# Block-sparse attention and a rational-activation MLP on one core: one written order for all engines through step 13, x split straight out of PSUM, and some pieces moved

## Chip, cores and metric

The kernel runs on 1 core of one Trainium2 chip. The metric is the device time of one execution in microseconds (us), median of the runs; lower is better. TensorE is called PE, VectorE DVE, ScalarE ACT, GpSimd POOL, and SyncE, which issues most transfers, SP.

## Reference

```python
B, H, S, D = 4, 8, 768, 64
block, window = 32, 16
k_sum = k.reshape(B, H, nb, block, D).max(axis=3)       # nb = 24 blocks
v_sum = v.reshape(B, H, nb, block, D).mean(axis=3)
scores_l = scale * q @ k.T, masked to |i - j| < window
scores_s = scale * q @ k_sum.T + log(block)
a = softmax(concat([scores_l, scores_s]))
attn = a @ concat([v, v_sum])
x = attn.transpose(0, 2, 1, 3).reshape(B * S, H * D)     # 3072 x 512
h = x @ w_in                                             # 512 -> 2048
g = (a0 + a1*h + a2*h*h + a3*h*h*h) / (1 + |b0|*|h| + |b1|*h*h + 1e-6)
return g @ w_out                                         # 2048 -> 512
```

## The kernel before

**Attention.** The 3072 rows are cut into 48 halves of 64 queries (`HQ`). One half covers all 8 heads, as 4 pairs (`NPAIR`). For a half, `scores` multiplies 64 queries with 96 neighbouring keys and 24 block keys, on quarters of the PE array (64x64); DVE adds the mask and takes the minimum (tile `ss`), ACT does four exponentials with their sums, DVE a reciprocal, POOL four multiplications (`ss<-ss,sm`). `turned` transposes on PE (tile `pt`), ACT or DVE copies to `pts`, and `values` multiplies with the values (tile `av`). From half 16 on, two halves go together (`both_scores`, `both_values`), and the transposition goes through memory (`crossed`).

**MLP.** Eight halves make a group of 512 rows, so there are six groups; a group has 16 steps, one for each 128 columns of the hidden layer. Step n does `moe1` (12 matmuls of 512 columns into tile `h`), the activation in `gelu`, and `moe2` of step n-3 (`LAG`; 12 matmuls into the four tiles `po`). Numbers are split in a high and a low part (`xh`/`xl`, the two parts of `wearly` and `w`, `gh`/`gl`), and three products of parts are added. In `gelu`, ACT makes a square, an absolute value and a line of `h`; DVE makes `tu` and `tq`; ACT does a logarithm and an exponential; DVE makes `gh` and the rest; POOL makes `gl`. `h` lies in a PSUM pool of two buffers (`ps_h`), which DVE's second product (`tu<-tu,cs,h`) reads last; scores, transposes and `av` of halves from 8 on, and ACT's squares of some steps, share another pool of two (`ps_a`).

**Weights.** They arrive packed; `w_split` unpacks them in the first group in five parts: ACT, POOL, DVE (`wr<-wr`), ACT's copy of the high part, and DVE's subtraction for the low part.

**The x of a group.** In group 0, `values` writes `xh` and `xl` from PSUM. In later groups ACT copies `av` to an fp32 tile `x` and `split`, at the first step of the group, makes `xh` (ACT) and `xl` (DVE) from it.

**Order.** `Kept` ties the instructions of an engine in the order of the program text while the engine is in `strict`. Before, PE, DVE, ACT and POOL are; SP is not. The text up to step 13 comes from three lists: `FIRST` (loads), `EARLY` (halves 0 to 7 and the first weights) and `STEP`, a pattern repeated for steps 0 to 13. From step 14 (`NSTRICT`) on, PE stays in the order of the text and the others are placed by the scheduler.

Of the kernel before, what the change touches and what calls it, by code (L numbers as in the profile page):

```python
# [8 lines left out]
F32 = mybir.dt.float32  # L9
# [38 lines left out]
FIRST = "K0 Q0 K1 K2 K3 Q1 S F W0 V0 V1 V6 V2 V4 V5 A9 W1 V7 V3 A8 W2 W3 G"  # L48
EARLY = "s0 s1 e0 s2 s6 e1 s3 s4 P0 v0 v1 e2 e3 e4 v2 v3 s5 P1 v4 v5 w0 w0 e5 w0 s7 P2 m0 w0 w0 C0 e6 P4 P3 e7 c2 c1 k8 p5 P6 C3 w1 P7 w1 c5 c4 w1 c6 c7 k9 w1 w1 w2 w2"
# [6 lines left out]
STEP = "k0 h3 w1 h2 h0 w2 P2 w1 w3 h3 g1 h0 g0 l0 q0 g1 g0 q0 h1 w2 u h0 a0 w3 v g0 h2"  # L56
# [4 lines left out]
def tile_kernel(ctx, tc, qw_in, kraw, kwin, vpad, vred, wio, a, b, cmask, cident, cavg, out):  # L61
# [36 lines left out]
    pe, dve, act, gps = Kept(nc.tensor), Kept(nc.vector), Kept(nc.scalar), Kept(nc.gpsimd)  # L98
# [11 lines left out]
    const.tile([P, 96], F32, name="shift")  # L110
    wearly = const.tile([P, NSTG, 2, 2, DM], F32R, name="wearly")
    const.tile([P, 32], F32, name="shift2")
# [6 lines left out]
    def setup():  # L119
# [5 lines left out]
        dve.tensor_scalar_mul(cs[:, 6:7], cs[:, 5:6], -1.0)  # L125
        dve.tensor_tensor(cs[:, 5:6], cs[:, 5:6], cs[:, 6:7], op=ALU.max)
        dve.memset(cs[:, 7:8], C1 * SH)

    ksum, vsum, att, x32, prods = {}, {}, {}, {}, {}
# [3 lines left out]
    def key_load(bi, pr):  # L133
        if pr == 0:
            ksum[bi] = sp.tile([P, NPAIR, NB], F32, tag="ks", name=f"ks{bi}", bufs=2)
        if bi == 0:
            nc.sync.dma_start(out=kres[:, pr, :], in_=kraw[bi, pr])
            kr = kres[:, pr, WIN:WIN + S]
        else:
            kr = stage.tile([P, S], F32, tag="st", name=f"kr{bi}_{pr}")  # L140
            nc.sync.dma_start(out=kr, in_=kraw[bi, pr, :, WIN:WIN + S])
        sums["k", bi, pr] = kr

    def key_sum(bi, pr):
        kr = sums.pop(("k", bi, pr))
        ins = dve.tensor_reduce(ksum[bi][:, pr, :], kr.rearrange("p (n k) -> p n k", k=BLK), axis=AX.X, op=ALU.max)
        if bi:
            tc.keep_in_program_order(ins)

    def value_load(bi, c):  # L150
# [3 lines left out]
        nc.sync.dma_start(out=vr, in_=vred[bi, c])  # L154
# [8 lines left out]
    def value_tiles(bi):  # L163
        vt = []
        for i, (n, pool, tag) in enumerate(((4, xp, "x" if bi else "xh"), (2, stage if bi else xp, "st" if bi else "xl"))):
            t = pool.tile([P, n, DM], F32, tag=tag, name=f"vf{bi}_{i}")
            nc.sync.dma_start(out=t, in_=vpad[bi, WIN + 4 * i * P:WIN + (4 * i + n) * P, :].rearrange("(t p) e -> p t e", p=P))
            vt += [t[:, k, :] for k in range(n)]
        return vt

    def value_average(av, vt, i):
        pe.matmul(av[:NK, :], avg[:, AVGW - NK - 4 * i:AVGW - 4 * i], vt[i], start=(i == 0), stop=(i == len(vt) - 1))

    def first_means(av):
        for t in vres[0:3]:
# [4 lines left out]
    def second_means(av):  # L180
        t = pp.tile([NK, DM], F32, tag="p", name="vn")
        act.copy(t[NKW:NK, :], av[NKW:NK, :])
        nc.sync.dma_start(out=vnext, in_=t[NKW:NK, :])

    def first_q(lo, hi):
        nc.sync.dma_start(out=qres[:, lo:hi], in_=qw_in[0, lo:hi].rearrange("j p r q -> p j r q"))

    def att_load(jj):
        bi, j = divmod(jj, NJ)
        nc.sync.dma_start(out=qw[jj % 2], in_=qw_in[bi, j])  # L190
        nc.sync.dma_start(out=kw[jj % 2][:, 0:NKC - 1], in_=kwin[bi, j])

    def key_blocks(jj):
        bi, j = divmod(jj, NJ)
        if j < 2 and bi > 0 or jj in (HPG, HPG + 1):
            dve.tensor_copy(kw[jj % 2][:, NKC - 1], ksum[bi])

    def both_scores(j0):

        tiles = [ps_a.tile([P, 512], F32, tag="a", name=f"sc{j0 + k}") for k in range(2)]  # L200
        for pr in range(NPAIR):
            for k in range(2):
                for e in range(2):
                    rows, q = slice(e * D, (e + 1) * D), e ^ k
                    pe.matmul(tiles[k][q * HQ:(q + 1) * HQ, pr * NK:(pr + 1) * NK], qw[k][rows, pr, :],
                              kw[k][rows, :, pr, :], start=True, stop=True)
        return tiles

    def scores(jj, early=False, sc=None):

# [475 lines left out]
```

## Time and profile before

| | us |
|---|---|
| median of 3 runs | 647.54 (644.51 to 650.65) |
| the profiled execution | 645.66 |
| its span | 643.6 |
| PE busy | 623.1 (97%) |
| DVE busy | 573.3 (89%) |
| ACT busy | 459.1 (71%) |
| POOL busy | 259.7 (40%) |

The span is the stretch that the trace covers; 2.06 us of the profiled execution lie around it. A busy PE counts also matmuls that run at a lower granted clock. A row of the timeline gives start, duration, engine, line, operation, output and inputs, count, and in brackets the idle time of the engine before it with what ended it. A row of the groups gives count, busy time, mean in ns, and idle time.

### The profile page before, as it was taken

The numbers are of one execution on the slowest core, as the hardware profiler recorded it, in microseconds if no ns is written. First come the engines' busy times: TensorE is split into PE (matmuls) and PEld (weight loads), VectorE is DVE, ScalarE is ACT, GpSimd is POOL, SyncE is SP. The second block draws the span as 40 slices with busy tenths as digits, with TensorE's granted clock in tenths as the row PEclk, the third lists the DMA queues.
The fourth block names the chain that finished last, engine by engine and source line by source line (L and its number), as shares of the span: only waits on it lengthen the run. The fifth ranks groups of instructions, "written<-read, shape, count | busy, mean of one in ns | idle before, by whom it ended". The sixth has DMA issues, their size and how long they took to land.

```text
span 643.6 us, 11833 instructions
## 1 busy us (share of the span) xinstructions
PE 623.1 (97%) x4068; PEld 497.2 (77%) x4068; DVE 573.3 (89%) x1152; ACT 459.1 (71%) x1032; POOL 259.7 (40%) x350
## 2 busy tenths in 40 slices
PE   8897999999999999999999999999999999999997
PEld 5564776777788887788887888888788888888886
DVE  5789999999988999998999999888988888898885
ACT  3987988978767667866767876767867756755552
POOL 1838569664243244333333245333334232222221
PEclk9997999999999999999999999999999999999999
DMA  8997854304443434244334343323233110100001
GB/s 314 301 346 253 256 190 148 134 27 133 144 145 125 143 111 141 66 141 143 115 110 132 92 134 105 93 72 121 66 130 124 31 64 1 44 22 1 0 2 65
DMA packets 51559, 77.00 MB, mean 120 GB/s; under 512 B 6068, under 2 KB 33076, under 8 KB 49580
## 3 DMA queue, kind: packets, MB, share of 16 engines
q1 hardware_dynamic: 50796, 75.80, 36.6%
q8 instruction: 32, 0.52, 0.3%
q10 hardware_dynamic: 576, 0.25, 0.2%
q0 software_dynamic: 128, 0.20, 0.1%
q14 instruction: 27, 0.22, 0.1%
HBM read 61.31 MB, written 14.73 MB: 118 GB/s over the span
## 4 chain that ended last, share of the span: by engine, by line
PE 62%; DVE 19%; POOL 7%; ACT 5%; issue 4%; DMA 2%; SPq 0%; DVEq 0%; POOLq 0%
PE po L88 28%; PE h L88 27%; DVE tu L88 7%; POOL ss L88 5%; DVE tq L88 4%; PE sc L88 3%; PE av L88 3%; DVE gh L88 2%; DVE xl L88 2%; ACT ta L88 1%; PE vf L88 1%; DVE ss L88 1%; DMA kres<-in_kraw_dram 1%; POOL gl L88 1%; ACT ss L88 1%
## 5 line engine op out<-in xcount | busy, mean ns | idle before, releaser
L88 POOL TENSOR_TENSOR gl<-tu,ta 128x512 fp32r<-128x512 f32 x96 | 129.4, 1348 | 311.3 <-DVE tu L88 156.9
L88 POOL TENSOR_SCALAR ss<-ss,sm 128x120 f32<-128x120 f32 x192 | 100.8, 544 | 61.8 <-DVE sm L88 59.1
L88 ACT ACTIVATE ta<-tq,cs 128x512 f32<-128x512 f32 x96 | 69.6, 725 | 77.1 <-DVE tq L88 75.8
L88 PE MATMUL po<-wearly,gh 128*128 128x512 f32 x384 | 121.6, 398 | 0.0
L88 PE MATMUL po<-w,gh 128*128 128x512 f32 x384 | 120.6, 395 | 0.0
L88 PE MATMUL h<-xh,wearly 128*128 128x512 f32 x384 | 97.2, 395 | 0.5 <-ACT xh L88 0.5
L88 PE MATMUL h<-xh,w 128*128 128x512 f32 x384 | 94.9, 389 | 0.0
L88 PEld LDWEIGHTS h<-xh,wearly 128*128 128x128 f32 x384 | 72.6, 189 | 17.6 <-issue 2.0
L88 PEld LDWEIGHTS h<-xh,w 128*128 128x128 f32 x384 | 72.0, 188 | 15.2 <-ACT x L88 0.2
L88 PEld LDWEIGHTS po<-w,gh 128*128 128x128 f32 x384 | 70.7, 188 | 15.3 <-issue 1.3
L88 PEld LDWEIGHTS po<-wearly,gh 128*128 128x128 f32 x384 | 70.0, 189 | 15.4 <-issue 1.7
L88 ACT ACTIVATE ss<-ss,sm 128x120 f32<-128x120 f32 x192 | 73.2, 386 | 12.1 <-DVE sm L88 12.0
L88 DVE SCALAR_TENSOR_TENSOR gh<-tu,cs,ta 128x512 fp32r<-128x512 f32 x96 | 72.6, 757 | 9.7 <-ACT ta L88 1.6
L88 DVE SCALAR_TENSOR_TENSOR tu<-tu,cs,tq 128x512 f32<-128x512 f32 x96 | 72.9, 759 | 2.4
L88 PE MATMUL po<-w,gl 128*128 128x512 f32 x192 | 74.9, 390 | 0.0
L88 PE MATMUL po<-wearly,gl 128*128 128x512 f32 x192 | 74.9, 390 | 0.0
L88 ACT ACTIVATE tu<-h,cs 128x512 f32<-128x512 f32 x96 | 74.8, 779 | 0.0
L88 DVE SCALAR_TENSOR_TENSOR tu<-tu,cs,h 128x512 f32<-128x512 f32 x96 | 71.4, 743 | 2.3
L88 DVE SCALAR_TENSOR_TENSOR tq<-tq,gh 128x512 f32<-128x512 f32 x96 | 66.7, 695 | 3.1
L88 ACT ACTIVATE ta<-h,cs 128x512 f32<-128x512 f32 x96 | 65.3, 680 | 3.0 <-POOL gl L88 2.9
L88 DVE TENSOR_TENSOR tu<-tu,h 128x512 f32<-128x512 f32 x96 | 65.0, 677 | 0.3 <-ACT tu L88 0.3
L88 ACT ACTIVATE ta<-ta 128x512 f32<-128x512 f32 x96 | 60.8, 634 | 2.8
(73 smaller groups left out, 918.2 us busy)
## 6 DMA issues: line engine op xcount, KB each, us to landing
wr<-in_wio_dram SPq DMA_DIRECT2D x15, 1024.0 KB
cross<-tb SPq DMA_DIRECT2D x32, 256.0 KB
vw<-in_vpad_dram SPq DMA_DIRECT2D x42, 192.0 KB
kw<-in_kwin_dram SPq DMA_DIRECT2D x40, 192.0 KB
pts<-cross SPq DMA_DIRECT2D x96, 64.0 KB
out_dram<-o SPq DMA_DIRECT2D x24, 256.0 KB
qw<-in_qw_dram SPq DMA_DIRECT2D x40, 128.0 KB
kr<-in_kraw_dram SPq DMA_DIRECT2D x12, 384.0 KB
```

The source lines that it names most:

```text
L88: out = getattr(self.engine, name)(*args, **kw)
```

## The change

1. `FIRST`, `EARLY` and `STEP` become one list, `TEXT`, whose tokens name single parts: `h8` the next part of half 8, `x2` the next third of `moe1` of step 2, `y1` the next quarter of `moe2`, `ga3` to `gk3` parts of the activation of step 3, `w`, `W`, `V`, `K` and so on weights and loads. SP is kept in the order of the text too.
2. In all groups `xh` and `xl` are written from PSUM, with two buffers each; `x` and `split` go.
3. `both_scores` also does halves 0 and 1, 2 and 3, 8 and 9 (`PAIRS`).
4. For the weights of steps 5, 7 and 8 (`MODE` e) the low part is made by ACT's negative of the high part and an adding transfer that POOL issues, in place of DVE's subtraction.
5. In half 3 (`SMODE` y) POOL subtracts the minimum, ACT does one exponential over all four pairs and DVE the sums.
6. In steps 1 to 15 `moe1` multiplies with the low weights last.

```diff
-FIRST = "K0 Q0 K1 K2 K3 Q1 S F W0 V0 ...
-EARLY = "s0 s1 e0 s2 s6 e1 s3 s4 P0 ...
-STEP = "k0 h3 w1 h2 h0 w2 P2 w1 w3 h3 g1 h0 ...
+TEXT = ("K0 K2 k0 Q0 K1 k1 k2 K3 k3 Q1 S0 F0 W0 ...
+PAIRS = "11001000"
+SMODE = "xxxyxxxxxxxxxxxx"
+ENG_P = "dddddaadaaadaaaa"
+ENG_X = "daadaaaaaaadaaaa"
+MODE = "ccccceceeccccccc"
...
@@ values
-        if g:
-            act.copy(x32[g][:, :, cols], av)
-        else:
-            xh, xl = x32[0]
-            (dve.tensor_copy if jj in by_dve else act.copy)(xh[:, :, cols], av)
-            yield
-            dve.tensor_tensor(xl[:, :, cols], av, xh[:, :, cols], op=ALU.subtract)
+        xh, xl = x32[g]
+        (dve.tensor_copy if ENG_X[jj] == "d" else act.copy)(xh[:, :, cols], av)
+        yield
+        dve.tensor_tensor(xl[:, :, cols], av, xh[:, :, cols], op=ALU.subtract)
...
@@ both_values
-        act.copy(x32[g][:, :, hh * HQ:(hh + 2) * HQ], av.rearrange("p r k q -> p r (k q)"))
-
-    def split(g):
...
-        for c in range(NCC):
-            act.copy(xh[:, c], x32[g][:, c])
-            dve.tensor_tensor(xl[:, c], x32[g][:, c], xh[:, c], op=ALU.subtract)
+        xh, xl = (x[:, :, hh * HQ:(hh + 2) * HQ] for x in x32[g])
+        av = av.rearrange("p r k q -> p r (k q)")
+        act.copy(xh, av)
+        dve.tensor_tensor(xl, av, xh, op=ALU.subtract)
...
@@ w_split
+            whole = packed.bitcast(F32)
+            if mode == "e":
+                act.copy(wt[:, 0], whole)
...
+            if mode != "a":
+                act.mul(wt[:, 1], wt[:, 0], -1.0)
...
+                gps.dma_start(out=wt[:, 1], in_=whole, accum_op=ALU.add)
...
@@ moe1
-        for i, x in ((0, xh), (1, xh), (0, xl)):
+        for i, x in ((0, xh), (0, xl), (1, xh)) if 0 < g * NFC + fc < NFC else ((0, xh), (1, xh), (0, xl)):
```

Three places show how the instructions move. The first is PE around `moe2` of step 2, with the transposes of half 10 (`pt_1010` before, `pt_1021` now). Before:

```order
L88 MATMUL h_5_987<-xl_464,wearly 128x512 x4
L88 MATMUL pt_1010<-ident,ss_870 120x128
L88 MATMUL po_0_844<-wearly,gh_2_757 128x512 x2
L88 MATMUL po_0_844<-wearly,gl_2_758 128x512
L88 MATMUL pt_1010<-ident,ss_870 120x128
L88 MATMUL po_1_845<-wearly,gh_2_757 128x512 x2
```

Now:

```order
L105 MATMUL po_2_819<-wearly,gh_2_753 128x512 x2
L105 MATMUL po_2_819<-wearly,gl_2_754 128x512
L105 MATMUL po_3_820<-wearly,gh_2_753 128x512 x2
L105 MATMUL po_3_820<-wearly,gl_2_754 128x512
L105 MATMUL pt_1021<-ident,ss_879 120x128 x4
L105 MATMUL h_6_1048<-xh_452,wearly 128x512 x4
```

The four transposes stood one ahead of each quarter of `moe2`; now they stand together behind all four. The second place is DVE at the start of group 1, in the activation of steps 14 and 15 (`tu_14`, `tq_15`). Before, it holds the four subtractions of `split`:

```order
L88 SCALAR_TENSOR_TENSOR tq_14_1689<-tq_14_1689,gh_14_1686 128x512
L88 TENSOR_TENSOR xl_1835<-x_817,xh_1834 128x512
L88 SCALAR_TENSOR_TENSOR tu_14_1690<-tu_14_1690,cs,tq_14_1689 128x512
L88 TENSOR_TENSOR xl_1835<-x_817,xh_1834 128x512 x2
L88 STREAM_TRANSPOSE tb_1804<-ss_1721 128x4x4x32
L88 TENSOR_TENSOR xl_1835<-x_817,xh_1834 128x512
L88 RECIPROCAL sm_1728<-sm_1728 128x4
L88 SCALAR_TENSOR_TENSOR tq_15_1789<-sq_15_1791,cs,ta_15_1788 128x512
```

Now a half's `xl` is made in the list, as here in step 3 for half 9:

```order
L105 SCALAR_TENSOR_TENSOR wr_697<-wr_697 128x1024
L105 SCALAR_TENSOR_TENSOR gh_3_811<-tu_3_815,cs,ta_3_813 128x512
L105 TENSOR_TENSOR xl_845<-av_917,xh_844 128x4x64
L105 SCALAR_TENSOR_TENSOR tq_3_814<-tq_3_814,gh_3_811 128x512
L105 SCALAR_TENSOR_TENSOR tu_3_815<-tu_3_815,cs,tq_3_814 128x512
```

Four subtractions of 512 columns ahead of step 16 became eight of 256 columns in steps 3 to 13. The third place is POOL in steps 2 to 5, with `gl` of steps 2 to 4 and the multiplications of halves 10 and 11. Before:

```order
L88 TENSOR_TENSOR gl_2_758<-tu_2_778,ta_2_776 128x512
L88 TENSOR_SCALAR wr_694<-wr_694 128x1024
L88 TENSOR_TENSOR gl_3_816<-tu_3_878,ta_3_876 128x512
L88 TENSOR_SCALAR wr_760<-wr_760 128x1024
L88 TENSOR_SCALAR ss_870<-ss_870,sm_871 128x120 x4
L88 TENSOR_TENSOR gl_4_917<-tu_4_965,ta_4_963 128x512
L88 TENSOR_SCALAR wr_828<-wr_828 128x1024
L88 TENSOR_SCALAR ss_957<-ss_957,sm_958 128x120 x4
```

Now:

```order
L105 TENSOR_SCALAR wr_697<-wr_697 128x1024
L105 DMA wearly<-wr_695 128x1024
L105 TENSOR_TENSOR gl_3_812<-tu_3_815,ta_3_813 128x512
L105 TENSOR_SCALAR wr_758<-wr_758 128x1024
L105 TENSOR_SCALAR ss_879<-ss_879,sm_880 128x120 x4
L105 TENSOR_TENSOR gl_4_913<-tu_4_916,ta_4_914 128x512
L105 TENSOR_SCALAR wr_831<-wr_831 128x1024
L105 DMA wearly<-wr_758 128x1024
L105 TENSOR_SCALAR ss_957<-ss_957,sm_958 128x120 x4
```

POOL's order is the same but for the two adding transfers, of step 5 ahead of `gl` of step 3 and of step 7 ahead of the multiplications of half 11.

More of the change, by code (lines that the diff above doesn't have):

```diff
@@ L207, in both_scores @@
-        return tiles
-    def scores(jj, early=False, sc=None):
-        bi, j = divmod(jj, NJ)
-        kt, qt = kw[jj % 2], qw[jj % 2] if jj >= HPG else qres[:, jj]
-        mt = mask[:, 0 if j == 0 else (2 if j == NJ - 1 else 1), :]
-        ready = sc is not None
-        if not ready:
-            sc = ps_o.tile([P, 512], F32, tag="o", name=f"sc{jj}") if early else ps_a.tile([P, 512], F32, tag="a", name=f"sc{jj}")
-        for pr in range(0 if ready else NPAIR):
-            if jj >= HPG:
+        early = j0 < HPG
@@ new lines, in gelu, with gelu_part, gelu_rest @@
+        return dict(a=a, b=b, c=c, d=d, e=e, f=f, i=i, j=j, k=k)
+    def gelu_part(step, what):
+        parts = gelus[step]
+        before = dict(a="", b="", c="a", d="c", e="b", f="e", i="df", j="i", k="j")[what]
+        assert not any(p in parts for p in before), (step, what)
+        parts.pop(what)()
+        if not parts:
+            del gelus[step]
+    def gelu_rest(step):
+        for what in "abcdefijk":
+            if what in gelus[step]:
+                gelus[step].pop(what)()
+        del gelus[step]
```

463 lines of the change are left out of this document (252 added, 211 removed), and 11 rows, old and new, of the table TEXT.

## Prediction

> **What bounds the kernel now.** I read the page first (busy shares, then the slices), then busy time by stage, then PE's waits, and last the timeline where those waits lie.
>
> ```profile
> span 643.6 us, 11833 instructions
> PE 623.1 (97%) x4068; PEld 497.2 (77%) x4068; DVE 573.3 (89%) x1152; ACT 459.1 (71%) x1032; POOL 259.7 (40%) x350
> 0.00:50.00 50.00, 45.52 (x509) 30.62 (x510) 35.93 (x130) 35.22 (x109) 21.52 (x46) 1.00 0.99 323
> 50.00:60.00 10.00, 6.41 (x17) 3.18 (x15) 9.93 (x16) 7.20 (x17) 8.91 (x9) 0.73 0.73 252
> 42.50:141.50 99.00, 91.35 (x571) 67.98 (x570) 96.99 (x176) 87.52 (x182) 68.12 (x58) 0.97 0.55 183
> 200.00:520.00 320.00, 316.85 (x2092) 258.68 (x2091) 288.76 (x608) 229.14 (x544) 119.35 (x194) 1.00 0.35 108
> ```
>
> PE is busy for 97% of the span, and from 200 us on for 99%: there the time is the number of matmuls, which the change leaves as it is. Only the start can give much. In it two engines are near their limit at once: from 42.5 to 141.5 us DVE is busy for 97.0 of 99 us and PE for 91.4. So waits of PE can go only as far as DVE keeps up, and DVE can come earlier only if its list starts earlier or gets shorter.
>
> ```profile
> PE pt L88 <- POOL ss L88: 7.3, 9, 2.2
> PE h L88 <- DVE xl L88: 1.3, 4, 0.4
> 52.52 0.32 PE L88 MATMUL pt<-ident,ss 128*120 128x128 f32 x1 [0.74 <-POOL ss L88]
> 56.88 3.62 PE L88 MATMUL vf<-vf,kres 128*120 128x512 f32 x4
> 59.52 3.31 PE L88 MATMUL h<-xh,wearly 128*128 128x512 f32 x8
> 68.52 1.98 PE L88 MATMUL h<-xh,wearly 128*128 128x512 f32 x8
> ```
>
> PE waits longest for the four multiplications of POOL ahead of a transpose (7.3 us in nine waits). The worst place is half 8: PE is there at 52.52 - 0.74 = 51.8 us, and goes on with other work at 56.88. Behind that pause eight matmuls of `moe1` take 3.31 us, where they take 1.98 us at 68.52: the granted clock of this stretch is 0.73.
>
> **The change, part by part.**
>
> *The start of DVE's list (parts 1, 3, 5).* DVE's idle time between 8 and 42 us, and the row at which its list becomes dense:
>
> ```profile
> L88 DVE CUSTOM_DVE_ANT_0 ss<-sc,mask 128x120 f32<-128x120 f32 x35 | 7.8, 278 | 3.5 <-PE sc L88 2.9 <-POOL ss L88 0.4 <-issue 0.2
> L88 DVE RECIPROCAL sm<-sm 128x4 f32<-128x4 f32 x8 | 1.4, 173 | 2.5 <-ACT sm L88 2.5
> L88 DVE COPY pts<-pt 120x512 f32<-120x512 f32 x7 | 4.7, 681 | 0.7 <-PE pt L88 0.7
> L88 DVE TENSOR_TENSOR xl<-av,xh 128x256 fp32r<-128x256 f32 x8 | 3.2, 419 | 0.6 <-ACT xh L88 0.5
> 21.07 1.14 ACT L88 ACTIVATE wr<-wr 128x1024 f32<-128x1024 f32 x1 [0.46 <-DMA wr<-in_wio_dram]
> 24.62 1.06 ACT L88 COPY vw<-vf 24x512 f32<-24x512 f32 x2
> 24.90 2.29 POOL L88 TENSOR_SCALAR ss<-ss,sm 128x120 f32<-128x120 f32 x4 [0.55 <-DVE sm L88]
> 27.25 2.72 POOL L88 COPY vr<-vw 24x512 f32<-24x512 f32 x3
> 29.92 1.18 POOL L88 COPY vlast<-vw 24x512 f32<-24x512 f32 x2
> 31.20 2.76 POOL L88 TENSOR_SCALAR ss<-ss,sm 128x120 f32<-128x120 f32 x8
> 37.51 2.12 PE L88 MATMUL h<-xh,wearly 128*128 128x512 f32 x8 [0.47 <-ACT xh L88]
> ```
>
> Without the wait for loads, DVE idles there 3.5 + 2.5 + 0.7 + 0.6 = 7.3 us. That is the most that a better order can give; the least is nothing, since the weights come with the DMA engines 99% busy. I follow POOL, on which the last halves hang. At 24.90 us it multiplies a half that was only just ready, slowly (2.29 us), and only then copies the block means (2.72 + 1.18 = 3.9 us, from 27.25). In the new order five halves' scores are done two pairs' worth earlier, half 3 takes one exponential, and so POOL can unpack the first weight when it lands (21.07, to 22.2) and multiply a half, whose exponentials are done, by 23.6. ACT copies the first means to POOL's source from 24.62 on, 0.53 us each; I take that one copy earlier, since the scores ahead of it come earlier. So POOL's copies begin at about 24.6, an estimate, and end at 28.5; three halves at 2.76 / 2 = 1.38 us follow (two before), so the last is ready at 32.6 against 33.96 before. Before, two halves came out of POOL at the end and 3.55 us passed to the first `moe1`; now one does, for which I take 2.9. The first `moe1` then starts at about 35.5 in place of 37.51, and DVE's list with it: **2.0 us earlier**. The pairing saves PE about as much again:
>
> ```profile
> 12.06 0.36 PE L88 MATMUL sc<-kres,qres 64*64 64x96 f32 x4
> 12.34 0.36 PE L88 MATMUL sc<-kres,qres 64*64 64x96 f32 x4
> 40.46 1.04 PE L88 MATMUL sc<-kw,qw 64*64 64x120 f32 x16
> 194.28 1.05 PE L88 MATMUL sc<-kw,qw 64*64 64x120 f32 x32
> ```
>
> A half's early scores are four of these 0.28 us pieces, 1.13 us, and 32 pieces of a pair take 1.05 us where 16 of a single half take 1.04. Three pairs save 1.13 + 1.13 + 1.04 = 3.3 us of PE. But PE waits behind them (half 8's transpose), so I count it at nothing beyond the 2.0.
>
> *Half 8.* POOL's row ahead of it:
>
> ```profile
> 52.09 4.48 POOL L88 TENSOR_SCALAR ss<-ss,sm 128x120 f32<-128x120 f32 x4
> ```
>
> It ends at 56.57. POOL's order up to here is unchanged (`gl` of step 0, a weight, half 8), and its head hangs on DVE. So the transposes come about 2.0 us earlier, at 54.5. PE is there at 51.8 less the 2.0 and the 1.04 of the third pair, at about 49. The pause stays, and with it the low clock.
>
> *Transposes behind `moe2`.* This is the largest term. The last one of the list, half 15:
>
> ```profile
> 131.98 0.32 PE L88 MATMUL pt<-ident,ss 128*120 128x128 f32 x1 [0.36 <-POOL ss L88]
> 135.28 1.98 PE L88 MATMUL h<-xh,w 128*128 128x512 f32 x8
> 129.66 4.59 POOL L88 TENSOR_SCALAR ss<-ss,sm 128x120 f32<-128x120 f32 x4
> ```
>
> Before, POOL released it at 131.98, and PE then still had four transposes and all of `moe2` before step 13 started at 135.28: 3.30 us. Now `moe2` runs ahead of the wait, and only the transposes are left, 0.5 us. With POOL 2.0 us earlier that gives 131.98 - 2.0 + 0.5 = 130.5: step 13 starts **4.8 us earlier**, of which 2.0 are the start and 2.8 the new place. PE gets there in time only if the same holds for halves 10 to 14, where between 1.4 and 2.8 us of `moe2` come ahead of the wait; that makes 3 to 5 us there by the same sum.
>
> Does DVE allow it? Step n+2 needs the buffer that DVE's second product of step n frees.
>
> ```profile
> 128.03 0.74 DVE L88 SCALAR_TENSOR_TENSOR tu<-tu,cs,h 128x512 f32<-128x512 f32 x1
> 158.03 0.75 DVE L88 SCALAR_TENSOR_TENSOR tu<-tu,cs,h 128x512 f32<-128x512 f32 x1
> 159.81 0.39 PE L88 MATMUL h<-xh,wearly 128*128 128x512 f32 x1
> ```
>
> Step 13 follows step 11's product (ends 128.77) by 6.5 us: room. The tight place is step 17, which starts 1.0 us after step 15's product. There DVE's shorter list counts:
>
> ```profile
> L88 DVE TENSOR_TENSOR wearly<-wr,wearly 128x1024 fp32r<-128x1024 f32 x7 | 8.5, 1217 | 0.1
> L88 DVE TENSOR_TENSOR xl<-x,xh 128x512 fp32r<-128x512 f32 x4 | 3.2, 818 | 0.0
> ```
>
> Gone are three subtractions of weights (3 x 1.22) and four of x (3.2); added are eight `xl` of 256 columns (3.2 by the row shown above), one `pts` copy (0.68) and one `xh` on DVE (by the price of an `xl`, 0.42). That is 6.9 gone and 4.3 added, 2.6 us less. Step 17 may start 1.0 + 2.0 + 2.6 = 5.6 us earlier: more than 4.8, so PE's sum decides.
>
> *x out of PSUM.* PE's waits for `xl` at the start of groups (1.3 us in four) end, since the last `av` of a group is written two steps ahead: **1.3 us**. ACT loses four copies per group, which lay beside matmuls and are worth nothing. What it may cost: DVE now waits for ACT's `xh` (0.6 us idle for eight in the row of `xl` above, so up to 0.6), and `av` keeps its buffer until DVE is through. I take nothing; the rival below prices it.
>
> *Adding transfers.* ACT's copy of an `av`, and the only transfers that POOL issued so far:
>
> ```profile
> L88 ACT COPY x<-av 128x256 f32<-128x256 f32 x8 | 2.9, 367 | 2.7 <-PE av L88 2.7
> L255 POOL DMA_DIRECT2D vw<-vs x4: 584/620/793, 250.8 to 390.7; - x4
> DMA to landing us min/median/max: 2.0/2.1/2.6
> 13.91 1.39 POOL L88 TENSOR_SCALAR ss<-ss,sm 128x120 f32<-128x120 f32 x4 [13.46 <-DVE sm L88]
> ```
>
> POOL needs 0.62 us for one, and 48 KB land in 2.1 us. The new ones carry 512 KB; by bytes that is 22 us, by count 2.1. ACT's negatives stand in steps 3, 5 and 6, the matmuls that need them last in steps 5, 7 and 8. At least one step lies between, and a step takes (135.28 - 59.52) / 10 = 7.6 us. So I take them as hidden, with a bound of 22 - 7.6 = 14.4 us for one. ACT's three negatives stand against the copies that it loses. POOL's four multiplications take 1.39 us alone and 4.59 us beside a full DVE, 3.3 times as long; stretched so, an issue takes 2.0 us. Only the one ahead of half 11 stands before a transpose, with 1.4 us of `moe2` ahead of it.
>
> The Trainium skill, "SBUF — State Buffer", section "SBUF: two separate sides", states that VectorE and GpSimd take a shared port pair as an exclusive lock, and that a transfer issued from GpSimd stalls while VectorE holds it, because its descriptors can't be written. The rows of 1.39 and 4.59 us agree on the lock; no run here shows it for a transfer. By that rule an issue takes at least the 2.0 us, and what comes ahead of half 11 may cost 1.4 us: the sum below would be 4.7 in place of 6.1.
>
> *Sum.* 4.8 + 1.3 = 6.1 us. 645.66 (span 643.6 and 2.06 around it) less 6.1 is 639.6, and I say **640**. The median of the runs, 647.54, is 1.9 above the profiled execution; by it the same sum gives 641.4. A measurement of this kernel can tell about 1% from no change, and the forecast lies just at that line.
>
> **Rivals.**
> 1. *The pause at half 8 goes.* If the new order brings DVE's start forward by most of the 7.3 us, say 6, the terms are 6 + 2.8 + 1.3 = 10.1 us, and the warmer clock adds 3.31 - 1.98 = 1.3: 634. For it: every engine has gaps before 42 us. Against: POOL's order at half 8 is the old one, and the weights arrive no sooner.
> 2. *The start gains nothing and PE's new room is not used*, because ACT or POOL keeps its pace (weights late, `xh` waited for, buffers of `ps_a` full). Then only 1.3 us are left: 644. For it: DVE at 97.0 of 99 us, and a list that is about as long. Against: the 2.8 us need no faster engine.
> 3. *Slower: the buffers of `av`.* In halves 8 to 15 `av` and the next transpose or scores share two buffers. Before, ACT freed `av` after 0.37 us; now DVE does, in order, and PE runs up to 6.5 us ahead of it. If DVE's row for it comes late, PE stands at each of the eight halves. At 1.75 us each that is 14 us less 6.1: 653.5. Slower than before from 6.1 / 8 = 0.8 us per half on. Against: the list puts `xl` only a few DVE rows behind `av`.
> 4. *An adding transfer lands late.* POOL issues late by 1.4 us three times, and from a landing time of 7.6 us on step 8 stops. With 4 us of waits: 644, like rival 2; at the bound of 14.4 us, 654. The lock of which the Trainium skill speaks (the page above) would be its cause.
>
> **Chances.** Forecast 0.50 (637 to 643), the first rival 0.15 (631 to 637), the second 0.20 (643 to 647), the third 0.10 (650 to 656), the fourth 0.05. The forecast reaches to both sides of the 1% line, so I give 0.32 of its 0.50 to faster. Faster by over 1%: 0.32 + 0.15 = 0.47; within 1%: 0.18 + 0.20 + 0.04 = 0.42; slower by over 1%: 0.11. The range 631 to 650 takes in all but the third rival and the far ends.
>
> **What would show it.** The first `moe1` at 35 to 36 us; half 8's transposes at about 54 us behind one pause of 5 to 6 us, clock below 0.8 there; PE's waits for `ss` from 11 to 15 below 2 us in all; step 13 at 130 to 131; no waits of `h` for `xl`. Wrong would be: a first `moe1` at 37 or at 32; waits of PE in halves 8 to 15 for `xl`; waits of steps 5, 7 or 8 for a transfer.

## The result, and the profile after

The changed kernel takes **650.27 us** (median, 648.33 to 653.51), the kernel before in the same runs 646.58. The ratio is 1.0056 with a 95% interval of 1.0038 to 1.0074: slower by 0.56%, where 640 was forecast and 631 to 650 given as the range. The profiled execution took 649.33 us with a span of 647.5, 3.9 us more than before.

The page's first lines, after:

```profile
span 647.5 us, 11826 instructions
PE 625.6 (97%) x4068; PEld 496.5 (77%) x4068; DVE 563.6 (87%) x1155; ACT 451.9 (70%) x1006; POOL 254.6 (39%) x354
```

The windows that answer to those of before; the columns are length, busy time (instructions) of PE, PE's weight loads, DVE, ACT and POOL, then the granted clock, the DMA share and GB/s:

```profile
0.00:50.00 50.00, 42.56 (x510) 28.30 (x511) 34.02 (x124) 32.77 (x93) 22.59 (x46) 1.00 0.92 308
50.00:60.00 10.00, 5.81 (x18) 3.38 (x17) 9.96 (x23) 9.83 (x28) 9.71 (x8) 0.91 0.92 320
42.50:141.50 99.00, 90.48 (x550) 67.66 (x550) 92.55 (x185) 87.97 (x181) 68.63 (x60) 0.98 0.62 196
200.00:520.00 320.00, 318.40 (x2085) 257.85 (x2084) 284.64 (x613) 224.02 (x534) 113.23 (x194) 1.00 0.34 107
```

Two things are to be seen. DVE, full before (97.0 of 99 us between 42.5 and 141.5), now idles 6.5 us there, and PE is no busier for it. And from 200 us on PE is busy for 318.4 us in place of 316.85 with seven matmuls fewer: the matmuls themselves have become longer, which no part of the prediction allows for.

PE's waits after (total, times, longest):

```profile
PE pt L105 <- POOL ss L105: 6.7, 8, 3.4
PE h L105 <- DVE xl L105: 1.5, 1, 1.5
```

The timeline after, at the places to which the prediction tied its steps (step 0, half 8, step 13 and POOL ahead of it):

```profile
38.31 1.89 PE L105 MATMUL h<-xh,wearly 128*128 128x512 f32 x7 [0.47 <-ACT xh L105]
53.48 0.32 PE L105 MATMUL pt<-ident,ss 128*120 128x128 f32 x1 [0.21 <-POOL ss L105]
57.24 0.32 PE L105 MATMUL pt<-ident,ss 128*120 128x128 f32 x1 [3.44 <-POOL ss L105]
58.11 0.81 PE L105 MATMUL pt<-ident,ss 128*120 128x128 f32 x2 [0.54 <-POOL ss L105]
136.48 0.33 PE L105 MATMUL pt<-ident,ss 128*120 128x128 f32 x1 [0.44 <-POOL ss L105]
136.56 1.18 PE L105 MATMUL h<-xh,w 128*128 128x512 f32 x4
132.30 4.12 POOL L105 TENSOR_SCALAR ss<-ss,sm 128x120 f32<-128x120 f32 x4
```

Step 0 starts at 38.31 (37.51 before; forecast 35.5), step 13 at 136.56 (135.28; forecast 130.5). Three distances make up the 4.1 us by which step 95, the last, starts later (629.96 against 625.90, from the timelines): 0.80 up to step 0; 0.62 from step 0 to step 15 (111.35 against 110.73 us); and 2.64 from step 15 to step 95. The last one is two things of opposite sign, as the experiments show: 3.85 lost by longer matmuls, 1.21 gained by x from PSUM. Only this third distance is clear of what kernels with the same instructions in the same order differ by. The experiments below add such kernels: with the new list (five profiles) step 0 starts at 38.31 to 41.49 us and steps 0 to 15 take 110.43 to 111.35; with the old one (four profiles) 37.51 to 39.62 and 109.45 to 110.89.

**The longer matmuls.** Groups of PE by form, after, with count, busy time and mean in ns:

```profile
L105 PE MATMUL po<-wearly,gh 128*128 128x512 f32 x384 | 121.7, 398 | 0.0
L105 PE MATMUL h<-xh,wearly 128*128 128x512 f32 x384 | 100.5, 401 | 0.5 <-ACT xh L105 0.5
L105 PE MATMUL po<-wearly,gl 128*128 128x512 f32 x192 | 75.9, 395 | 0.0
L105 PE MATMUL h<-xl,wearly 128*128 128x512 f32 x192 | 53.0, 398 | 0.0
```

The same groups before:

```profile
L88 PE MATMUL po<-wearly,gh 128*128 128x512 f32 x384 | 121.6, 398 | 0.0
L88 PE MATMUL po<-wearly,gl 128*128 128x512 f32 x192 | 74.9, 390 | 0.0
L88 PE MATMUL h<-xh,wearly 128*128 128x512 f32 x384 | 97.2, 395 | 0.5 <-ACT xh L88 0.5
L88 PE MATMUL h<-xl,wearly 128*128 128x512 f32 x192 | 52.7, 392 | 1.4 <-DVE xl L88 1.3
```

In three of the four forms with `wearly`, the weights of steps 0 to 7 of a group, a matmul takes 5 or 6 ns more; with `w`, the weights of the other steps, the means of the four forms move by 2 ns at most. Such means also hold matmuls at a lower clock. The distance of two steps is the sharper measure. In the last group, where nothing waits, two neighbours start at these times in the timeline of before:

```profile
571.50 1.98 PE L88 MATMUL h<-xh,wearly 128*128 128x512 f32 x8
576.94 1.98 PE L88 MATMUL h<-xh,wearly 128*128 128x512 f32 x8
```

And after:

```profile
574.82 2.03 PE L105 MATMUL h<-xh,wearly 128*128 128x512 f32 x8
580.41 2.03 PE L105 MATMUL h<-xh,wearly 128*128 128x512 f32 x8
```

A step of 5.44 us has become one of 5.59. The clock is 1.00 in both, and the instructions are the same. What differs is the place. Two lines of the diff, which the section on the change left out because they compute nothing, were tiles that nobody uses:

```diff
-    const.tile([P, 96], F32, name="shift")
     wearly = const.tile([P, NSTG, 2, 2, DM], F32R, name="wearly")
-    const.tile([P, 32], F32, name="shift2")
```

`shift2` takes 128 bytes of each partition. Without it, by the built programs' addresses, `wearly` starts at 352 modulo 512 bytes and `xh`, `xl`, `gh`, `gl` at 224; with it all of them start at the same place modulo 2048.

### The profile page after: what moved, and what is told of

It reads as the page before. It is cut to its first block, busy times and chain, and to the rows that moved or that the text cites. A ratio compares the mean times of both kernels' runs of the same rounds, so it can differ in the third digit from the quotient of the medians.

```text
span 647.5 us, 11826 instructions
## 1 busy us (share of the span) xinstructions
PE 625.6 (97%) x4068; PEld 496.5 (77%) x4068; DVE 563.6 (87%) x1155; ACT 451.9 (70%) x1006; POOL 254.6 (39%) x354
## 4 chain that ended last, share of the span: by engine, by line
PE 72%; DVE 14%; ACT 5%; POOL 5%; issue 3%; DMA 1%; SPq 0%; DVEq 0%; POOLq 0%; ACTq 0%
PE po L105 32%; PE h L105 32%; DVE tu L105 5%; PE sc L105 3%; DVE tq L105 3%; POOL ss L105 3%; PE av L105 3%; DVE gh L105 2%; ACT ta L105 1%; ACT ss L105 1%; DMA kres<-in_kraw_dram 1%; POOL gl L105 1%; PE vf L105 1%; DVE ss L105 1%; ACT wr L105 1%
## 5 line engine op out<-in xcount | busy, mean ns | idle before, releaser
L105 POOL TENSOR_TENSOR gl<-tu,ta 128x512 fp32r<-128x512 f32 x96 | 127.4, 1327 | 331.9 <-DVE tu L105 190.2
L105 POOL TENSOR_SCALAR ss<-ss,sm 128x120 f32<-128x120 f32 x192 | 93.9, 508 | 41.4 <-DVE sm L105 40.4
L105 PE MATMUL h<-xh,wearly 128*128 128x512 f32 x384 | 100.5, 401 | 0.5 <-ACT xh L105 0.5
L105 ACT ACTIVATE ta<-tq,cs 128x512 f32<-128x512 f32 x96 | 69.7, 726 | 41.5 <-DVE tq L105 39.0
L105 PE MATMUL h<-xh,w 128*128 128x512 f32 x384 | 97.1, 391 | 1.5 <-DVE xl L105 1.5
L105 ACT ACTIVATE ss<-ss,sm 128x120 f32<-128x120 f32 x188 | 71.7, 385 | 16.1 <-DVE sm L105 15.9
L105 ACT ACTIVATE sq<-h 128x512 f32<-128x512 f32 x53 | 30.9, 584 | 49.7 <-PE h L105 49.4
```

What stands on the lines that cost most here:

```text
L105: out = getattr(self.engine, name)(*args, **kw)
```

## The experiments

Each ratio is that to the kernel before in the same runs. It is worked out from the single runs and is not the quotient of the medians given here, so the two can differ by some tenths of a per cent. "The changed kernel with the 128 bytes" (`a_gap`) is the base of several.

### The place of wearly

**The 128 bytes put back** (`a_gap`):

```diff
     wearly = const.tile([P, NSTG, 2, 2, DM], F32R, name="wearly")
+    const.tile([P, 32], F32, name="shift2")
```

> The changed kernel with one unused tile of 128 bytes per partition put back behind wearly, so that wearly and the tiles it is multiplied with (xh, xl, gh, gl) again start at the same place modulo 512 bytes; no instruction changes. Theory (place in SBUF): the twelve matmuls of moe1 and of moe2 with wearly take 2.72 us again in place of 2.80, 0.155 us less per step, and with 8 such steps in 6 groups the time falls by about 7.4 us, to 643. Rival (two buffers of x, or DVE's and ACT's other access times, slow those matmuls): the time stays at 650 and the twelve at 2.80.

646.07 us, ratio 0.9973 (0.9945 to 1.0000). By its timeline the step is 5.44 us again:

```profile
572.61 1.98 PE L105 MATMUL h<-xh,wearly 128*128 128x512 f32 x8
578.05 1.98 PE L105 MATMUL h<-xh,wearly 128*128 128x512 f32 x8
```

Its groups:

```profile
L105 PE MATMUL po<-wearly,gh 128*128 128x512 f32 x384 | 120.0, 394 | 0.0
L105 PE MATMUL po<-wearly,gl 128*128 128x512 f32 x192 | 74.8, 390 | 0.0
```

The theory holds, but at 4.2 us by the medians, 5.4 by the ratios (1.0056 and 0.9973) and 3.85 by the traces (from step 15 to step 95, 476.45 against 480.30 us), not at 7.4. In the last group, where nothing waits, the place costs 1.35 us (81.60 against 82.95 from step 80 to step 95). In groups 4, 3 and 2 it costs 1.29, 0.63 and 0.90, in group 1 nothing. Part of the difference is that PE waits for DVE at some steps of these groups, and that a PE that comes later waits less: between 155 and 545 us these waits are 3.6 us in `a_gap` and 2.1 in the changed kernel. The rest is open.

**Both unused tiles taken out of the kernel before** (`b_nofill`), and **only the first** (`b_nofirst`):

```diff
-    const.tile([P, 96], F32, name="shift")
     wearly = ...
-    const.tile([P, 32], F32, name="shift2")      (only in b_nofill)
```

> The kernel before without its two unused tiles, the 384 bytes per partition ahead of wearly and the 128 bytes behind it; no instruction changes. Theory (place in SBUF): wearly then stands 128 bytes off the tiles it is multiplied with, as in the changed kernel, so the twelve matmuls go from 2.72 to 2.80 us and the time rises by about 7.4 us, to 654. Rival: no change, 646.6.

> The kernel before without the 384 bytes ahead of wearly only; the 128 bytes behind it stay. All later tiles move down by 384 bytes together. Theory (only the distance between the operands counts): no change, 646.6, twelve matmuls at 2.72 us. Rival (the place of wearly itself, modulo 2048 bytes, counts): the time rises by up to 7.4 us, as in the kernel without both.

Without both: 649.99 us, ratio 1.0051 (1.0020 to 1.0082). Without the first alone: 646.22 us, 1.0004 (0.9977 to 1.0031). So most of the change's loss can be had on the kernel before by deleting lines that compute nothing, and moving all tiles together does nothing. In all kernels of this section the traces show the same instructions in the same order on PE, DVE, ACT and POOL as in the kernel that they are made from.

**256 bytes ahead of wearly in the changed kernel** (`a_ahead`: all tiles move, the distance stays):

```diff
+    const.tile([P, 64], F32, name="ahead")
     wearly = ...
```

> The changed kernel with an unused tile of 256 bytes per partition ahead of wearly: all tiles move up together, and wearly stays 128 bytes off the others. Theory (only the distance between the operands counts): no gain, 650, twelve matmuls at 2.80 us. Rival (the place of wearly itself counts): the time falls by up to 7.4 us.

650.50 us, ratio 1.0063 (1.0038 to 1.0089): as without. It is the distance between the operands that counts, not the place of `wearly`.

**Other distances**, one execution each: 64 and 256 bytes behind `wearly` in the changed kernel (64 bytes off; 128 bytes off on the other side), and 640 in the kernel before (512 bytes off).

> The changed kernel with an unused tile of 64 bytes behind wearly, so that wearly stands 64 bytes off the tiles it is multiplied with (128 in the changed kernel, 0 with 128 bytes). One look for the mean of the matmuls with wearly: 401 ns (xh) and 395 ns (gl) at 128 bytes off, 398 and 390 at 0. Theory (any distance other than 0 costs): 400 and 395. Rival (only a distance from 128 bytes on costs): as at 0.

> The changed kernel with an unused tile of 256 bytes behind wearly, so that wearly stands 128 bytes off the tiles it is multiplied with on the other side. One look for the mean of the matmuls with wearly. Theory (the distance counts, whatever its sign): 401 ns (xh) and 395 ns (gl), as without the tile. Rival (the side counts): 398 and 390, as with 128 bytes.

> The kernel before with 640 bytes behind wearly in place of 128, so that wearly stands 512 bytes off the tiles it is multiplied with. One look for the mean of the matmuls with wearly: before 395 (xh), 390 (gl), 392 ns (xl); with 128 bytes off 401, 395, 396. Theory (the distance counts modulo 512 bytes or less): as before. Rival (modulo 1024 or 2048 bytes): as with 128 bytes off.

The group of `xl` with `wearly` at 64 bytes:

```profile
L105 PE MATMUL h<-xl,wearly 128*128 128x512 f32 x192 | 53.2, 399 | 0.0
```

And at 512:

```profile
L88 PE MATMUL h<-xl,wearly 128*128 128x512 f32 x192 | 52.4, 391 | 1.1 <-DVE xl L88 1.0
```

64 bytes cost nearly what 128 do, the sign does not matter, and 512 bytes are as good as none. The time from step 80 to step 95, worked out from each timeline, parts all these kernels in two:

| kernel | bytes apart, modulo 512 | step 80 to step 95, us |
|---|---|---|
| before | 0 | 81.60 |
| before, without the first unused tile | 0 | 81.60 |
| before, 512 bytes apart | 0 | 81.60 |
| before, without both | 128 | 82.95 |
| changed | 128 | 82.95 |
| changed, 256 bytes ahead | 128 | 82.95 |
| changed, 64 bytes behind | 64 | 82.89 |
| changed, 256 bytes behind | 128, other side | 82.95 |
| changed, 128 bytes behind | 0 | 81.60 |

Distances below 64 bytes and between 128 and 512 were not tried.

### Transposes behind moe2

**Taken back inside the new list** (`g_pt`, halves 10 to 15). In the list, the token of the four transposes becomes four tokens:

```diff
-    ... y2 y2 y2 gi4 y2 w7 h10 ...
+    ... h10 y2 h10 y2 h10 y2 gi4 h10 y2 w7 ...
```

> The changed kernel with the 128 bytes behind wearly (646.1 us), and the transposes of halves 10 to 15 put back as before, one ahead of each quarter of moe2 (half 9 stays behind moe2). Theory of the prediction: the place behind moe2 is worth 2.8 us at step 13, so step 13 comes 2.8 us later after step 0 and the time is about 649. Rival (the pace of steps 3 to 13 is set by what DVE and ACT do in order, and what PE no longer waits for transposes it waits for elsewhere): from step 0 to step 15 it stays at 110.9 us, the time within 1 us of 646.

652.39 us, ratio 1.0105 (1.0082 to 1.0129); from step 0 to step 15 it takes 118.2 us in place of 111.0. By this run the new place is worth 6 us, more than the 2.8 forecast. But it was taken back in a list whose other engines are written around it, so the edit was also made alone.

**Alone on the kernel before** (`b_pt`):

```diff
-                po = second_layer(step, queue, po, pt)
+                po = second_layer(step, queue, po, None)
                 lead(pt, True)
```

> The kernel before with one edit: the four transposes of halves 9 to 15 stand together behind the four quarters of moe2, as in the change, and not one ahead of each. Nothing else changes. The prediction's sum for this edit: step 13 comes 2.8 us earlier after step 0 (95.0 in place of 97.8 us) and the time falls to 643.4. Rival (PE's waits ahead of the transposes of halves 10 to 15 are 3.2 us in all, and where PE waits less there it only comes sooner to DVE, which is full): less than 1 us, 645.5 to 646.5. Second rival (later transposes make ACT's and DVE's copies and the product behind them late): slower, 647 or more.

647.48 us, ratio 0.9996 (0.9962 to 1.0030): nothing. POOL and PE at half 15 in its timeline:

```profile
129.62 4.60 POOL L88 TENSOR_SCALAR ss<-ss,sm 128x120 f32<-128x120 f32 x4
133.61 0.49 PE L88 MATMUL pt<-ident,ss 128*120 128x128 f32 x3
134.28 0.32 PE L88 MATMUL pt<-ident,ss 128*120 128x128 f32 x1 [0.18 <-POOL ss L88]
134.35 2.10 PE L88 MATMUL h<-xh,w 128*128 128x512 f32 x8
```

The last transpose of half 15 in the timeline of before:

```profile
134.47 0.27 PE L88 MATMUL pt<-ident,ss 128*120 128x128 f32 x1
```

POOL multiplies at the same time as before (129.62; 129.66 before). Its four multiplications release the four transposes one by one until 134.2, and the last transpose stands at 134.28 where it stood at 134.47. What comes off is the last quarter of `moe2` behind it: step 13 starts at 134.35, 0.93 earlier (1.1 after step 0, which is 0.16 later here). That this is the edit's is read from the rows alone: in the kernel before with `wearly` 512 bytes apart, whose instructions and order are the old ones, step 13 comes 1.3 us earlier after step 0 too. At step 17 only 0.14 is left (159.67 against 159.81). PE waits for DVE's `xl` just ahead of it (0.40 us before), and DVE runs at its old pace:

```profile
156.59 0.50 PE L88 MATMUL h<-xl,wearly 128*128 128x512 f32 x1 [1.05 <-DVE xl L88]
```

### What the new list waits for

**Half 8's product moved** (`g_av8`, from `a_gap`):

```diff
-    ... x3 x3 h10 x3 w4 y0 h9 y0 W8 h10 A12 h8 y0 ...
+    ... x3 x3 h8 h10 x3 w4 y0 h9 y0 W8 h10 A12 y0 ...
```

> The changed kernel with the 128 bytes behind wearly (646.1 us), and only the product av of half 8 moved on PE, from behind the first quarter of moe2 of step 0 and the scores of half 10 to a place ahead of the last third of moe1 of step 3. Theory (DVE and ACT, which are now held in one written order, stand at half 8's xh and xl for 2.4 and 4.0 us, and this uses up what the transposes gain): both waits fall below 1 us, steps 5 and 6 come 1 to 2.4 us earlier after step 0, and the time falls to 644 to 645. Rival (DVE's wait was slack): from step 0 to step 15 it stays at 110.9 us, 646.

In the timeline of `a_gap`, ACT and DVE stand behind half 8; the third row is a wait of DVE soon after, for ACT's line of `h`:

```profile
67.02 0.37 ACT L105 CAST xh<-av 128x256 fp32r<-128x256 f32 x1 [3.99 <-PE av L105]
67.42 0.42 DVE L105 TENSOR_TENSOR xl<-av,xh 128x256 fp32r<-128x256 f32 x1 [2.40 <-ACT xh L105]
70.19 0.69 DVE L105 TENSOR_TENSOR tu<-tu,h 128x512 f32<-128x512 f32 x1 [0.96 <-ACT tu L105]
```

`av` of half 8 is behind a quarter of `moe2` and the scores of half 10 on PE; ACT's `xh` is next in ACT's order and waits 3.99 us for it, DVE's `xl` 2.40. With the product ahead, step 0 to step 15 takes 109.52 us in place of 110.96 (110.43 at the least in the five profiles with this order), as expected, and part of the gain goes at once to the next wait. The last third of `moe1` of step 8, in the timeline of `g_av8`:

```profile
100.76 1.20 PE L94 MATMUL h<-xh,w 128*128 128x512 f32 x4 [1.06 <-DMA w<-wr]
```

And that transfer, in the view of tile `w`:

```profile
DMA to landing us min/median/max: 6.0/6.0/6.0
```

PE is there before it has landed, 6.0 us after its issue. The times (644.81 us, ratio 0.9981, 0.9961 to 1.0001) can't tell this from `a_gap`.

**That transfer brought forward** (`g_av8_w8`) or **taken away** (`g_av8_c8`):

```diff
-    ... h11 w8 x7 gd6 x7 y3 A14 h13 y3 x7 w8 h11 w8 h13 ...     (g_av8)
+    ... h11 w8 x7 w8 w8 gd6 w9 w9 x7 y3 A14 h13 y3 x7 h11 h13 ...     (g_av8_w8)
-MODE = "ccccceceeccccccc"
+MODE = "cccccececccccccc"     (g_av8_c8)
```

> The changed kernel with the 128 bytes and with half 8's av moved (644.8 us), and the adding transfer of step 8 brought forward: ACT's negative and POOL's issue come ahead of the logarithm of step 6, and the first unpacking of step 9's weight behind it. Theory (with half 8 out of the way PE reaches step 8 before that transfer has landed, 6.0 us after its issue, and waits 1.06 us): the wait goes and the time falls by up to 1.1 us, to 643.7. Rival (the wait only takes the place of another one on DVE's list): no change, 644.8.

> The changed kernel with the 128 bytes and half 8's av moved (644.8 us), and the low part of step 8's weight made by DVE's subtraction again, without the adding transfer, which lands 6.0 us after its issue. Theory (that transfer holds step 8): PE's wait of 1.06 us goes, DVE gets 1.2 us more, which it has idle: 109.5 us from step 0 to step 15 fall to about 108.5, the time to 643.8. Rival (DVE's list is what the steps wait for): 1.2 us more, 646.

Brought forward: 646.15 us, ratio 0.9975 (0.9944 to 1.0006). PE still waits, and step 0 to step 15 takes 110.90 us, so that the gain of half 8 is gone. The wait in its timeline:

```profile
102.97 1.19 PE L94 MATMUL h<-xh,w 128*128 128x512 f32 x4 [1.19 <-DMA w<-wr]
```

The issue is 2.2 us earlier after step 0, but the landing takes longer, in the same view:

```profile
DMA to landing us min/median/max: 8.9/8.9/8.9
```

The trace's packets show where: the first one moves 3.95 us after the issue, in `g_av8` 1.87. SP issues three loads in the 1.0 us ahead of the issue here, where in `g_av8` its last load is issued 2.6 us ahead; whether these loads hold the transfer is not shown.

Taken away: 650.67 us, ratio 1.0044 (1.0016 to 1.0072), 5.9 us above `g_av8`, where the rival said 1.2. This run doesn't give the price of the subtraction: of the 6.9 us by which step 95 starts later in its timeline, 1.1 are lost ahead of step 0 and 1.1 in step 2, which the edit doesn't touch, and 3.6 behind step 15, where the scheduler placed DVE's, ACT's and POOL's instructions in another order. So the first edit ends as its rival said, with no change. In the second the theory fails, but that DVE has no 1.2 us to spare is shown only by the next run, where nothing else moves.

**All three transfers taken back** (`g_sub`) and **two of the pairs** (`g_nopair`), from `a_gap`:

```diff
-MODE = "ccccceceeccccccc"
+MODE = "cccccccccccccccc"     (g_sub)
-PAIRS = "11001000"
+PAIRS = "00001000"     (g_nopair)
```

> The changed kernel with the 128 bytes behind wearly (646.1 us), and the three adding transfers taken back: DVE's subtraction makes the low part of the weights of steps 5, 7 and 8 as before, three times 1.22 us. Theory (the transfers are hidden, and DVE's list is what the steps up to 13 wait for): DVE's list gets 3.7 us longer and the time rises by up to 3.7 us, to 648 to 650. Rival (the transfers and ACT's three negatives, 1.06 us each, are what costs): the time falls to 643 to 645. Third: no change, if DVE has that much idle time in waits.

> The changed kernel with the 128 bytes behind wearly (646.1 us), and the scores of halves 0 and 1, 2 and 3 each for itself again, at the places of the list where the parts of those halves stand. Theory (the pairs make PE wait 2.06 us for two free PSUM buffers and bring vf and so ACT's copies of the means later): the first moe1 comes up to 1.5 us earlier than the 38.3 to 39.6 us of the kernels with the pairs, the time falls to about 645. Rival (the pairs save PE 2.3 us ahead of step 0): the first moe1 comes up to 2.3 us later, 648.

`g_sub`: 652.01 us, ratio 1.0086 (1.0058 to 1.0114). Step 0 to step 15 takes 115.06 us, 4.1 more, for 3.7 us of subtractions, and from step 15 on nothing changes (476.44 us). `g_nopair`: 649.46 us, ratio 1.0054 (1.0033 to 1.0075), with the first `moe1` at 42.30 in place of 39.60 (38.1 to 41.5 in the other profiles of the list). So the transfers do free DVE, and the pairs do pay, in this list.

### x from PSUM

**Part 2 alone on the kernel before** (`b_x`):

```diff
-        if g:
-            act.copy(x32[g][:, :, cols], av)
-        else:
-            xh, xl = x32[0]
+        if True:
+            xh, xl = x32[g]
             (dve.tensor_copy if jj in by_dve else act.copy)(xh[:, :, cols], av)
...
-        act.copy(x32[g][:, :, hh * HQ:(hh + 2) * HQ], av.rearrange("p r k q -> p r (k q)"))
+        act.copy(xh, av)
+        dve.tensor_tensor(xl, av, xh, op=ALU.subtract)
```

> The kernel before with part 2 of the change alone: xh and xl of all groups written from PSUM, two buffers each, no x and no split; for the room, the output tiles have two buffers of their own and two shared ones as in the changed kernel, the first unused tile goes and POOL's transfers get 2 KB less; wearly keeps its place relative to the tiles it is multiplied with. Prediction: 1.3 us less, by PE's waits for xl at the starts of groups, 645. By the steps of the changed kernel with the 128 bytes: the starts of the groups gain 3.9 us, and 2.7 us come back where av waits for DVE in the middle of groups, 1.2 us less in sum. Rival (DVE holds av so long that PE loses more than it gains): 646 to 650.

651.42 us, ratio 1.0078 (1.0047 to 1.0108): the rival. From step 0 to step 15 it takes 114.41 us in place of 110.73; from there on it is 1.16 us faster, as in the changed kernel. In the first stretch DVE and ACT wait in their orders (waits of both between 38 and 150 us):

```profile
DVE xl L88 <- ACT xh L88: 3.2, 3, 1.9
ACT xh L88 <- PE av L88: 4.1, 5, 2.0
```

DVE had no such wait there before. It is busy for 109.2 us between steps 0 and 15 (108.0 before) and idle for 5.2 (2.7): 1.2 us more work (the eight `xl` are 3.4, and a few other rows now fall behind the stretch), and 2.5 of standing, on an engine that was full.

**The same, but halves 8 to 15 the old way** (`b_x2` on the kernel before; `g_x1` on `a_gap`; `g_av8_x1` on `g_av8`):

```diff
+        if g:
+            act.copy(x32[g][:, :, cols], av)
+            yield
+            return
         xh, xl = x32[g]
...
+        if step == NFC:
+            with tc.high_priority(offset=60):
+                split(g)
```

> The kernel before with part 2 for the halves from 16 on only; halves 8 to 15 go through an fp32 tile and split as before (its xl takes the place of group 0's, as before). Theory: the 3.7 us of steps 0 to 15 are gone again (110.7), the starts of groups 2 to 5 gain as with part 2 everywhere, and av held by DVE costs up to 2 us in group 1: 645 to 646.5. Rival (the 651.4 us of part 2 alone come from the output tiles or from the smaller room for POOL's transfers): 650 to 651.

> The changed kernel with the 128 bytes behind wearly (646.1 us), and group 1's x made the old way: ACT copies the av of halves 8 to 15 to an fp32 tile (in the second buffer of xl), and at step 16 ACT makes xh and DVE xl from it; groups 2 to 5 stay on PSUM. Theory (part 2 in halves 8 to 15 costs 3.7 us on DVE's list, as in the kernel before with part 2 alone): from step 0 to step 15 it takes 107 to 108.5 us in place of 111, the start of group 1 costs 0.7 us again, and the time falls by about 2 to 3 us, to 643 to 644. Rival (the list as a whole takes that long, whatever DVE does for x): 646 to 647.

> The same with half 8's av ahead of the last third of moe1 of step 3. Theory (with no xl on DVE's list half 8's av holds up ACT alone): no more than 1 us below the run without that move. Rival (half 8's av matters by itself): 1.4 us less, as it did from step 0 to step 15 with xl on the list.

`b_x2`: 647.65 us, ratio 1.0032 (1.0004 to 1.0061), and step 0 to step 15 is back at 110.65 us: the 3.7 us are those eight halves. It was expected at 645 to 646.5 and is not faster than before: what it gains at the starts of groups, and 2.5 us more, it loses ahead of steps 22, 30 and 31. But `g_x1` takes 110.83 us there, `a_gap` 110.96, `g_av8_x1` 109.74, `g_av8` 109.52. In the new list that theory falls: with an fp32 copy it is still ACT that stands for half 8's `av` (3.4 us at most in place of 4.0), and DVE now for ACT. Whether moving half 8's product helps without `xl` (1.1 us between steps 0 and 15) can't be told from the 0.9 us by which equal orders differ. Their times, 651.46 (1.0084, 1.0056 to 1.0113) and 651.72 (1.0088, 1.0055 to 1.0120), fit neither theory nor rival. They are lost later: the stretches ahead of steps 16, 22, 30 and 31, which the scheduler orders, take 0.9 to 2.7 us more each than in `a_gap`.

## Why the prediction was wrong, step by step

1. **The start** (2.0 us earlier forecast, 0.8 later came). The step that failed is "I take that one copy earlier". PE, ACT and POOL in the timeline after:

```profile
18.07 0.30 PE L105 MATMUL sc<-kres,qres 64*64 64x96 f32 x2 [2.06 <-issue]
26.02 1.06 ACT L105 COPY vw<-vf 24x512 f32<-24x512 f32 x2 [2.46 <-PE vf L105]
26.75 1.73 POOL L105 COPY vr<-vw 24x512 f32<-24x512 f32 x3 [0.35 <-ACT vw L105]
29.70 5.17 POOL L105 TENSOR_SCALAR ss<-ss,sm 128x120 f32<-128x120 f32 x12
```

   PE has the pairs' scores ahead and stands 2.06 us at a score tile (the trace names no cause); the averages come later, so ACT's copy of the means starts at 26.02 in place of 24.62 and POOL's at 26.75, where 24.6 was forecast. The multiplications behind them end at 34.87, not at 32.6, and from there to the first `moe1` it is 3.44 us, not 2.9. In seven profiles with the old list the first `moe1` starts at 37.3 to 39.6 us, in twelve with the new one at 38.1 to 41.5 (42.3 without the pairs); the medians are 37.7 and 39.2.

2. **Half 8.** The pause stays, as forecast: 0.21 + 3.44 + 0.54 = 4.2 us up to 58.1, though not one of 5 to 6 us with the transposes at 54. The clock does not stay low: 0.91 there, forecast below 0.8.

3. **Transposes behind moe2** (2.8 forecast, 0.93 measured alone at step 13, 0.14 left at step 17). This is the term that carried the forecast, and it was mis-sized in the prediction's own rows. The release at 131.98 is that of the first of four transposes. POOL's row, quoted there, runs from 129.66 for 4.59 us: it releases the fourth at 134.25, and behind that only 1.0 us of PE was left before step 13. So 0.9 was there to be had, and in the changed kernel that is what came: step 13 follows POOL's last multiplication (132.30 and 4.12, 136.42) by 0.14 us. But POOL ends it 98.1 us after step 0 in place of 96.7, not earlier. The mark set for this step was met all the same: PE's waits for `ss` in halves 11 to 15 fall from 3.2 to 1.1 us (0.46, 0.16 and 0.44). Waits that go are no gain where the engine that feeds them keeps its pace.

4. **DVE's list** (2.6 us shorter forecast). The window from step 0 to step 15, before (DVE is the third busy time):

```profile
37.51:148.24 110.73, 103.08 (x656) 76.81 (x657) 107.99 (x210) 98.05 (x201) 70.51 (x62) 0.97 0.57 188
```

And after:

```profile
38.31:149.66 111.35, 102.83 (x657) 77.34 (x657) 104.16 (x219) 98.14 (x197) 71.12 (x64) 0.98 0.59 188
```

   DVE has 3.8 us less to do (107.99 to 104.16) and idles 4.4 us more (110.73 less 107.99 is 2.7; 111.35 less 104.16 is 7.2). "The list puts `xl` only a few DVE rows behind `av`" and "up to 0.6" for the wait for ACT's `xh` were wrong: one `xl` alone waits 2.4 us (in `a_gap`) with all of DVE's list behind it, since half 8's product comes late on PE. By moving that product step 0 to step 15 takes 1.4 us less, 0.9 below the fastest profile of the same order. Why the rest of the list is no faster, with transfers and pairs that each cost 3 to 6 us when taken back, is not settled: `g_pt` and `b_pt` (6 us and nothing for the same edit) show that taking a part out of a list written around it doesn't give its price.

5. **x from PSUM** (1.3 forecast, 1.2 measured from step 15 on). The sum is right by two errors that cancel: the starts of groups 1 to 4 gain 3.9 us, three times what the waits for `xl` showed, and 2.7 come back in the middle of groups (by the distances of the steps in `a_gap` and before). The longest wait there, in the timeline after:

```profile
249.93 2.14 PE L105 MATMUL h<-xh,w 128*128 128x512 f32 x8 [1.53 <-DVE xl L105]
```

   At that place `av`, which lies in the buffers of `h`, is held until DVE's `xl`. That is the third rival's mechanism, at step 31 and not in halves 8 to 15. And what this part adds to DVE's order in steps 3 to 13 was counted at no more than 0.6 us; alone it costs 3.7 (`b_x`).

6. **Adding transfers.** Hidden, as taken, in the changed kernel; they land 4.7 to 5.7 us after the issue for 512 KB, nearer to the 2.1 by count than to the 22 by bytes. The views of the tiles `wearly` and `w` after:

```profile
DMA to landing us min/median/max: 4.7/5.0/5.4
DMA to landing us min/median/max: 5.7/5.7/5.7
```

   Their issues in the timeline after:

```profile
71.79 1.11 POOL L105 DMA_DIRECT2D wearly<-wr  x1 [0.88 <-ACT pts L105]
87.57 0.90 POOL L105 DMA_DIRECT2D wearly<-wr  x1 [0.28 <-POOL wr L105]
```

   An issue takes 0.9 to 1.1 us, not the 2.0 that the forecast worked out from a full DVE. The Trainium skill, "SBUF — State Buffer", section "SBUF: two separate sides", has such a transfer stall while VectorE holds the shared port, and names operations in a two-port mode as those that do. DVE is busy for 17.0 of the 18 us around the three issues, but the trace doesn't show which of its operations are in that mode; so the price isn't seen at the issue here, and the rule is neither confirmed nor refuted. A late landing, the fourth rival, is what `g_av8` shows, at 1.06 us, once PE comes earlier.

7. **Not in the sum at all: the place of wearly**, 3.9 us by the trace. Without it the changed kernel is at 0.9973 (0.9945 to 1.0000), and its median, 646.07, is that of the kernel before in the same runs, 646.22: not the forecast's 640 either. It is the second rival's mechanism (the start gains nothing, PE's room isn't used). Of that rival's 1.3 us the traces show 1.2 from step 15 on; the times can't tell them from nothing. That the change is slower, and not level, is due to the line `shift2`.

## What to carry to other kernels

Read a release off the last of the instructions that it feeds, not the first: four multiplications that release four transposes over 4.6 us leave only what stands behind the fourth. Where an engine is full, a move on another engine is worth what it takes out of the full one's line, waits in its order included. And compare the addresses of a matmul's operands before and after a change of tiles: a line that computes nothing was worth 4 us here, as much as the whole loss.

## What the runs showed of the hardware

The 24 matmuls of a step take 5.59 us in place of 5.44, 6 ns or 2.8% each, when the two operands in SBUF start 64 or 128 bytes apart modulo 512 and not at the same place or 512 bytes apart. It happens with `wearly` as the stationary operand (`moe1`) and as the moving one (`moe2`). Why is open. The Trainium skill, "SBUF — State Buffer", section "SBUF: two separate sides", states that TensorE never waits on another engine for SBUF; these runs don't speak against that, since the clock, the instructions and the other engines' work were the same with and without the unused tiles, but they show that its rate is not independent of addresses.
